# One fused kernel of attention, expert layer and dense layer on one core: all weight splits on VectorE, quarter rows stored in the dense layer's second half, weight conversions in tighter marks, the third split behind the logits' copies

## The chip, the cores and the metric

The kernel runs on one core of a Trainium2 chip. The metric is the device time of one execution in microseconds (us): the median of three timed runs. A separate profiled execution gives the trace from which all rows below are taken. The engines are named as the profile names them: PE is TensorE (with its weight loads as PEld), DVE is VectorE, ACT is ScalarE, POOL is GpSimd, and SP is SyncE, which here only issues transfers.

## The reference, cut to what matters

```python
# attention with a sigmoid: B=4, H=12, S=448, D=64
scores = q @ k.T / sqrt(D) - log(S)
x = (sigmoid(scores) @ v) -> rows of 768, N = 1792 tokens
# expert layer: E=8 experts, 768 -> 1024 -> 768, one expert per token
logits = x @ w_gate; e = argmax(logits); g = softmax(logits)[e]
y = g * (relu(x @ w1[e]) @ w2[e])
# dense layer: 768 -> 2048 -> 768
out = relu(y @ w_in) ** 2 @ w_out
```

All arithmetic is at fp32 accuracy. The kernel gets it from three fast matmuls for each product: a matrix a is split into a high part h, its value rounded to the matmul's type, and a low part l = a - h, and a product is h·h + h·l + l·h.

## The kernel before

**Attention.** 24 units (four batches, six pairs of heads each) run one after the other. In unit n PE computes the scores in four chunks, ACT the sigmoids, and PE the product with v of unit n-1 (`av_step`), its transposes (`rows`, called by `extras`) and, in every third unit, gate logits (`logits`, `token_logits`). DVE splits the next unit's q and k (`split_qk`, tiles qkh and qkl), copies results out of PSUM (xT, ls, lg) and converts the dense layer's weights.

**Conversion of the dense weights.** They come as 64-bit floats in 16 pieces of 128x1536 and are turned into 32-bit floats on DVE by `narrow(m, k)`: step 0 loads, steps 1 to 4 make the bits (step 2 also has an absolute value on ACT, tile ca or whc, which step 4 reads), and a write to DRAM follows on POOL's queue (w_d for m < 8; t_d for the eight pieces of the second layer, behind steps 5 and 6, which form sums for a seven-product block scheme). Pieces 0 to 8 (`PRE` = 9) are converted in the attention: `convert(n, half)` is called twice in each unit. Pieces 9 to 15 are converted in the dense layer's first half by `rest()`, which is called four times in each `layer1` and has one buffer wlc for its result, so step 1 of the next piece waits until the write of the last one has landed.

**Expert layer.** Routing (`head`, `counts`, `slots`, `late_places`, ...) puts the tokens into 15 slots of 128 rows with one expert each (`NBASE`) and four quarters of 32 rows. A slot takes eight weight chunks c: four for the first matrix (`up`), four for the second (`down`). PE works through them in order. Once it has done chunk c of slot s, `next_chunk(s, c)` splits chunk c of slot s+1: h on ACT, l on DVE, and for c = 7 (`POOL_W`) and s < 13 l on POOL. The four transposed parts of the hidden layer are split by `htrans` (ACT hh, DVE hl); PE needs hl for its third matmul of `down(4)`. Slot 0's chunks are split by `split_first` (chunks 0 to 3) and by `opening`.

**Quarters.** Their results wait in yq_d and are copied into y_d, at row numbers that the routing computes, by `quarter_rows()`: four times a register load and a transfer of 32x769 on POOL's queue. As the rows aren't known in advance, such a transfer waits for all earlier reads and writes of y_d.

**Dense layer.** Two blocks of tokens (8 tiles, then 6). Each runs 16 calls of `layer1` (first half), then seven products of four steps g each with weights from t_d (second half). y_d's tiles are loaded by `load_y` on SP and transposed by `trans_y`; those of block 1 are loaded from g = 16 of block 0 on.

The order on each engine is the program's order (the schedule is manual); every engine and every DMA queue takes its instructions in that order and stands still while the first of them waits.

Of the kernel before, what the change touches and what calls it, by code (L numbers as in the profile page):

```python
# [10 lines left out]
F32 = mybir.dt.float32  # L11
# [6 lines left out]
ALU = mybir.AluOpType  # L18
# [25 lines left out]
NBASE = NTL + 1  # L44
NCOL = FS + LC
QB = 3
CH = 1536
# [5 lines left out]
DH = DM // 2  # L53
PRODS = (0, 2, 6, 5, 7, 4, 3)
PRE = 9
POOL_W = (7,)
TWO30 = 2.0 ** 30
TINY = 2.0 ** -15 * 1.125

# [1 line left out]
def f32(ap):  # L61
    return ap.bitcast(F32)
# [3 lines left out]
def moe_kernel(ctx: ExitStack, tc: tile.TileContext, qk, v, wg, wm, w2, out):  # L66
    nc = tc.nc
# [119 lines left out]
    def head(t0, t1):  # L187
        n = t1 - t0
        l, q, m_, me_ = lg[:, t0:t1], eq[:, t0:t1], m[:, t0:t1], me[:, t0:t1]
        mb = m_.unsqueeze(2).to_broadcast([CP, n, E])  # L190
        V.tensor_reduce(out=m_, in_=l, op=ALU.max, axis=AX.X)
        V.tensor_tensor(q, l, mb, op=ALU.is_equal)
        V.tensor_tensor(z[:, t0:t1], l, mb, op=ALU.subtract)
        V.tensor_tensor(q, q, rev[:CP].unsqueeze(1).to_broadcast([CP, n, E]), op=ALU.mult)
        V.tensor_reduce(out=me_, in_=q, op=ALU.max, axis=AX.X)
        V.tensor_tensor(oh.rearrange("p e t -> p t e")[:, t0:t1], q, me_.unsqueeze(2).to_broadcast([CP, n, E]), op=ALU.is_equal)
        V.tensor_tensor_scan(cum[:CP].rearrange("p e t -> p (e t)"), seg[:CP].rearrange("p e t -> p (e t)"), ohz[:CP].rearrange("p e t -> p (e t)"), 0.0,
                             op0=ALU.mult, op1=ALU.add)
# [120 lines left out]
    def rtile(k, name, dt=F32):  # L319
        return rawp.tile([128, 2 * CH], dt, tag=f"raw{k}", name=name)  # L320
# [4 lines left out]
    with ExitStack() as actx:  # L325
# [83 lines left out]
        def token_logits():  # L409
            if not ready_l:  # L410
                return
            b, ls = ready_l.pop(0)
            o = lgT[b][:CP, S:S + NC * E].rearrange("p (c e) -> p c e", c=NC)
            for c in range(NC):
                nc.tensor.matmul(o[:, c], ls[:GJ * GW, c * CP:(c + 1) * CP], pick[:GJ * GW], start=True, stop=True, skip_group_check=True)
            nc.vector.tensor_copy(lg[:, b * NC:(b + 1) * NC, :], o)
# [19 lines left out]
        cvp = cctx.enter_context(tc.tile_pool(name="cvp", bufs=2, reuse_waits="tile"))  # L436
        conv = {}

        def convert(n, half):
            if n < 2:  # L440
                if half == 0:
                    fetch(n)
                return
            m, o = divmod(n - 2, 2)
            if m < 0 or m >= PRE:
                return
            if o == 0 and half == 0:
                conv[m] = (conv[m], cvp.tile([128, 2 * CH if m >= 8 else CH], F32, tag="dst", name=f"cd{m}"),
                           cvp.tile([128, CH], F32, tag="ab", name=f"ca{m}", bufs=1))
            narrow(m, 1 + 2 * o + half, *conv[m])  # L450
            if o == 1 and half == 0 and m + 2 < PRE:
                fetch(m + 2)
            if o and half:
                narrow(m, 5, *conv[m])
            if (m == PRE - 1 if o and half else o == 0 and half == 0 and m > 0):
                last = m if o else m - 1
                narrow(last, 6, *conv.pop(last))

        def fetch(m):
            conv[m] = cvp.tile([128, 2 * CH], F32, tag="src", name=f"cs{m}")  # L460
            narrow(m, 0, conv[m], None, None)
# [6 lines left out]
                    fin_av(b, j, po)  # L468
                    done.append((b, j))

        def split_w(src, h, l, pool=False):
            nc.scalar.activation(h, src, AF.Copy)  # L472
            (nc.gpsimd if pool else nc.vector).tensor_tensor(l, src, f32(h), op=ALU.subtract)  # L473

        def split_first(c):
            split_w(chunk0(c), wh[c], wl[c])
            if c == 1:
                for w, l in (("wh", wh), ("wl", wl)):
                    both = wpair(w, F32R, f"{w}23")
                    l.extend([both[:, :CH], both[:, CH:]])  # L480
# [3 lines left out]
        for n, (b, j) in enumerate(units):  # L484
            if n + 3 < len(units):
                loaded[n + 3] = load(*units[n + 3])
            if n == 0:
                nc.sync.dma_start(out=gw[:, :, :E], in_=wg)
                nc.sync.dma_start(out=x_d[0:128, :].rearrange("p (a n) -> p a n", a=8), in_=zero.unsqueeze(1).to_broadcast([128, 8, DM // 8]))
                nc.sync.dma_start(out=g_d[:FR].rearrange("(a t) b -> a (t b)", a=1), in_=zero[0:1, :FR])  # L490
            if n >= len(units) - 4:
                rawb.append(rtile(n % 4, f"raw{n}"))
                raw.extend([rawb[-1][:, :CH], rawb[-1][:, CH:]])
            if n == last_n - 3:
                cctx.close()
                w1p = ctx.enter_context(tc.tile_pool(name="w1p", bufs=1, side="right", reuse_waits="tile"))
                wh, wl = ([w1p.tile([128, CH], F32R, tag=f"{w}{c}", name=f"{w}{c}") for c in range(2)] for w in ("wh", "wl"))
                first = wpair("wl", F32, "first")
            if n == last_n - 2:
                regs(0)  # L500
                reload(0, 0)
                reload(0, 1)
            if n == last_n - 1:
                reload(0, 2)
                reload(0, 3)
            if n == last_n:
                reload(0, 4)
                reload(0, 5)
            vr = loaded.pop(n)[1]
            if n + 1 < len(units):  # L510
                terms[n + 1] = split_qk(n + 1)
            r = terms.pop(n)
            po = ps_a.tile([128, 512], F32, tag="po", name=f"po_{b}_{j}")
            cur = [score(b, j, 0, r), score(b, j, 1, r)]
            due = len(ready_l)
            if done:
                logits(*done[0])
            av_step(0)
            av_step(1)
            av_step(2)  # L520
            convert(n, 0)
            cur.append(score(b, j, 2, r))
            cur.append(score(b, j, 3, r))
            if due or n == last_n - 4:
                token_logits()
            if n == last_n - 3:
                p1 = ps_e.tile([128, 512], F32, tag="lgT", name="p1")
                pn1, prk1 = p1[:, :E], p1[:CP, E:E + FR * E].rearrange("p (e t) -> p e t", e=E)
                pr1 = p1[:, E + FR * E:E + FR * E + 2 * FS]
                counts(pn1, prk1, FR)  # L530
            if done:
                extras()
            if n == last_n - 2:
                pick_rows(pr1, Bt1, FR)
            av_step(3)
            if n == last_n - 4:
                head(0, FR)
            convert(n, 1)
            if n == last_n - 3:
                early_expert(pn1, prk1)  # L540
                spots(range(FR))
            if n == last_n - 2:
                early_rest(pr1)
                xg = {s: early_gather(s) for s in range(FS)}
            if n == last_n - 1:
                split_first(0)
            if n == last_n:
                split_first(1)
                split_first(2)
            prev = (b, j, cur, vr, po)  # L550
        av_step(0)
        av_step(1)
# [8 lines left out]
        logits(*done[0])  # L561
        extras()
        token_logits()
        head(FR, NR)
        split_first(3)
        nc.scalar.activation(ez[:, :FR], z[:, :FR], AF.Exp)
# [87 lines left out]
    with ExitStack() as mctx:  # L654
# [25 lines left out]
            nc.tensor.matmul(ps, lh, rl, start=False, stop=False)  # L680
            nc.tensor.matmul(ps, ll, rh, start=False, stop=last)  # L681

        def split_m(c, pool):
            split_w(raw[c], mh[c], ml[c], pool=pool)

        def next_chunk(s, c):
            if s + 1 < NBASE:
                split_m(c, c in POOL_W and s < NBASE - 2)
            if s + 2 < NBASE:
                reload(s + 2, c)  # L690
            if s == NBASE - 2:
                load_next(min(c + 1, AHEAD))
# [319 lines left out]
    for bi, (t0, P) in enumerate(blocks):  # L1012
# [52 lines left out]
        for c, h in steps:  # L1065
            layer1(c, h)
            if bi == 0 and c < 2 and h == 0:
                for t in (2 * c, 2 * c + 1):
                    trans_y(0, 1, t, yns.pop(t), yT[1], ps_q, ("pq", "pq"))
                    if t + 2 < P:  # L1070
                        yns[t + 2] = load_y(0, 1, t + 2, xgp, 2, "xg")
                if c == 0:
                    quarter_rows()
            seen[c] = seen.get(c, 0) + 1
            if seen[c] == 2:
                second(c)
                advance()
            if len(seen) == 8 and sum(seen.values()) == 15:
                split_s(0)
                split_s(1)  # L1080
        if bi == 0:
            ob = [rtile(k, f"ob{k}") for k in (2, 3)]
        obs = [[ob[h][:, p * DM:(p + 1) * DM] for p in range(P)] for h in range(2)]
        po = {}
# [118 lines left out]
```

## Time and profile before

| | us |
|---|---|
| median of three timed runs | 977.54 (977.25 to 978.46) |
| the profiled execution, its own time | 974.72 |
| its span, first to last instruction | 972.9 |
| PE busy | 939.6 (97% of the span) |
| DVE busy | 634.5 (65%) |
| ACT busy | 551.0 (57%) |
| POOL busy | 132.8 (14%) |

Attention fills the span up to about 184 us, the expert layer up to about 506 us, and the dense layer the rest. The profiled execution is 2.82 us below the median of the timed runs. "Busy" of PE counts matmuls as they overlap, so 97% doesn't mean that the array runs at its peak; what counts for a change here is where PE stands still, and at which clock it runs afterwards.

### The profile page before, as it was taken

The page shows a single profiled execution, that of the slowest core. Times are in us where ns is not written, and L with a number is a line of the kernel's source. Part 1 is how long each engine was busy: PE and PEld are TensorE (multiplying, and loading weights), DVE is VectorE, ACT ScalarE, POOL GpSimd, SP SyncE. Part 2 cuts the span into 40 slices and gives each one's busy share as a digit, 9 for nine tenths or more (in the row PEclk, how much of TensorE's full clock was granted, in tenths as well). Part 3 has the DMA queues.
Part 4 walks back from the last instruction along what each step waited for, and adds up shares of the span by engine and source line. Part 5 has one row for each costly group of instructions (what it writes and reads, how often), then busy time and mean ns, then how long its engine had stood idle before and what let it go on. Part 6 is the DMA issues. An engine that isn't in the chain of part 4 may idle for free. (4 is left out here: it accounts for less than half of the span.)

```text
span 972.9 us, 15008 instructions
## 1 busy us (share of the span) xinstructions
PE 939.6 (97%) x5869; PEld 786.3 (81%) x5869; DVE 634.5 (65%) x694; ACT 551.0 (57%) x667; POOL 132.8 (14%) x118
## 2 busy tenths in 40 slices
PE   7999999998999999999989799999999999999996
PEld 3555554587888888888878588889999999999996
DVE  2777777789876777777755486647866612228762
ACT  4766665756777777777854255455435344446540
POOL 1000001024523333222200100000000210000002
PEclk9999999999999999999999899999999999999998
DMA  8798868571577879593545555463233532223312
GB/s 283 255 339 300 297 231 313 182 298 37 174 281 276 333 252 387 202 408 117 202 158 193 189 208 202 187 226 99 98 123 123 192 115 65 66 66 105 123 33 97
DMA packets 52511, 190.62 MB, mean 196 GB/s; under 512 B 8082, under 2 KB 18962, under 8 KB 50386
## 3 DMA queue, kind: packets, MB, share of 16 engines
q1 hardware_dynamic: 34290, 152.77, 43.8%
q0 software_dynamic: 6928, 31.08, 8.4%
q10 hardware_dynamic: 11216, 5.75, 2.1%
q8 instruction: 48, 0.79, 0.3%
q14 instruction: 29, 0.24, 0.1%
HBM read 203.33 MB, written 36.98 MB: 247 GB/s over the span
## 5 line engine op out<-in xcount | busy, mean ns | idle before, releaser
L473 DVE TENSOR_TENSOR wl<-raw,wh 128x1536 fp32r<-128x1536 f32 x98 | 195.5, 2000 | 59.7 <-ACT wh L472 56.3
L472 ACT ACTIVATE wh<-raw 128x1536 fp32r<-128x1536 f32 x110 | 163.0, 1483 | 2.7 <-PE ph L681 0.6
L377 ACT ACTIVATE a<-sc,bias_s 128x896 f32<-128x896 f32 x96 | 82.6, 911 | 56.6 <-PE sc L373 56.3
L1036 ACT ACTIVATE r<-pp 128x512 f32<-128x512 f32 (+1 forms) x64 | 34.9, 545 | 100.5 <-PE pp L1032 100.2
L1134 PE MATMUL pq<-wrh,sh 128*128 128x384 f32 x264 | 89.1, 337 | 0.3 <-DVE ob L1095 0.3
L1135 PE MATMUL pq<-wrl,sh 128*128 128x384 f32 x264 | 88.7, 336 | 0.0
L1136 PE MATMUL pq<-wrh,sl 128*128 128x384 f32 x264 | 88.7, 336 | 0.0
L681 PE MATMUL py<-wh,hl 128*128 128x384 f32 x240 | 81.8, 341 | 5.5 <-DVE hl L706 5.5
L679 PE MATMUL py<-wh,hh 128*128 128x384 f32 x240 | 85.2, 355 | 0.0
L680 PE MATMUL py<-wl,hh 128*128 128x384 f32 x240 | 81.3, 339 | 0.0
L473 DVE TENSOR_TENSOR wrl<-raw,wrh 128x1536 fp32r<-128x1536 f32 x30 | 52.7, 1758 | 36.1 <-ACT wrh L472 36.1
L679 PE MATMUL ph<-wh,xh 128*128 128x512 f32 x180 | 74.9, 416 | 0.0
L472 ACT ACTIVATE wrh<-raw 128x1536 fp32r<-128x1536 f32 x30 | 44.4, 1483 | 48.6 <-PE pq L1136 43.3
L681 PE MATMUL ph<-wh,xl 128*128 128x512 f32 x180 | 71.2, 396 | 0.0
L680 PE MATMUL ph<-wl,xh 128*128 128x512 f32 x180 | 71.1, 395 | 0.0
L1057 DVE TENSOR_TENSOR sl<-h,sh 128x1024 fp32r<-128x1024 f32 (+1 forms) x56 | 59.8, 1086 | 8.7 <-ACT sh L1056 8.6
L1044 DVE TENSOR_TENSOR h<-h,h 128x512 f32<-128x512 f32 (+1 forms) x16 | 10.0, 624 | 80.7 <-ACT h L1039 80.7
L383 PE MATMUL po<-a,qkv 128*64 128x448 f32 x288 | 59.6, 548 | 0.0
L473 POOL TENSOR_TENSOR wl<-raw,wh 128x1536 fp32r<-128x1536 f32 x12 | 42.0, 3497 | 128.5 <-ACT wh L472 128.4
L1056 ACT ACTIVATE sh<-h 128x1024 fp32r<-128x1024 f32 (+1 forms) x56 | 51.5, 943 | 13.5 <-PE pq L1135 8.0
L1000 POOL DMA_INDIRECT out<-ob,idx x14 | 13.7, 978 | 314.7 <-DVE ob L1095 286.0
L1030 PE MATMUL pp<-hy,wrh 128*128 128x512 f32 (+1 forms) x132 | 49.5, 375 | 6.8 <-ACT r L1036 6.8
(290 smaller groups left out, 2192.2 us busy)
## 6 DMA issues: line engine op xcount, KB each, us to landing
raw<-in_wm SPq DMA_DIRECT2D x110, 768.0 KB
qraw<-in_wm SPq DMA_DIRECT2D x32, 768.0 KB
raw<-t_d SPq DMA_DIRECT2D x28, 768.0 KB
cs<-in_w SPq DMA_DIRECT2D x9, 1536.0 KB
raw<-w_d SPq DMA_DIRECT2D x16, 768.0 KB
qkv<-in_qk SPq DMA_DIRECT2D x23, 480.0 KB
whc<-in_w SPq DMA_DIRECT2D x7, 1536.0 KB
t_d<-wlc POOLq DMA_DIRECT2D x7, 1536.0 KB, 7.7
```

Of the source, the lines that this page charges most:

```text
L377: nc.scalar.activation(a[:, :n], ps[:, :n, :S], AF.Sigmoid, bias=bias_s, scale=1.0 / math.sqrt(D))
L383: nc.tensor.matmul(po[64 * h:64 * h + 64, :S], vr[:, 128 * c + 64 * h:128 * c + 64 * h + 64], a[:, h], start=(c == 0), stop=False, skip_gr ...
L472: nc.scalar.activation(h, src, AF.Copy)
L473: (nc.gpsimd if pool else nc.vector).tensor_tensor(l, src, f32(h), op=ALU.subtract)
L679: nc.tensor.matmul(ps, lh, rh, start=first, stop=False)
L680: nc.tensor.matmul(ps, lh, rl, start=False, stop=False)
L681: nc.tensor.matmul(ps, ll, rh, start=False, stop=last)
L1056: nc.scalar.activation(sh[:, :2 * N], src, AF.Copy)
L1057: V.tensor_tensor(sl[:, :2 * N], src, f32(sh[:, :2 * N]), op=ALU.subtract)
L1134: nc.tensor.matmul(po[p][:, :DH], lh, wc[:, w0:w0 + DH], start=(q == 0 and kk == 0 and o in (0, 2, 5)), stop=False, **fl)
L1135: nc.tensor.matmul(po[p][:, :DH], lh, wcl[:, w0:w0 + DH], start=False, stop=False, **fl)
L1136: nc.tensor.matmul(po[p][:, :DH], ll, wc[:, w0:w0 + DH], start=False, stop=(q == 3 and kk == 1), **fl)
```

## The change

Four edits:

1. `next_chunk` gives no split to POOL any more. Chunk 7's l is made on DVE, as that of the other chunks; these are 12 instructions.
2. `quarter_rows()` is called after the last `layer1` of block 0, where it was called after the first.
3. The conversion steps of pieces 0 to 8 in the attention follow a list of marks, two for each unit. Step 1 of every even piece but the first shares a mark with step 4 of the piece before it, steps 5 and 6 of piece 8 have a mark each, and the last mark lies in unit 18 (before: unit 19). The number of steps is the same.
4. `split_first(2)` moves from the end of unit 23 to behind `token_logits()`, ahead of the second `head`.

```diff
+        marks = []
+        for i in range(PRE):
+            for k in range(1, 5):
+                if i and i % 2 == 0 and k == 1:
+                    marks[-1].append((i, k))
+                else:
+                    marks.append([(i, k)])
+        marks.extend([[(PRE - 1, 5)], [(PRE - 1, 6)]])
+
         def convert(n, half):
             if n < 2:
                 if half == 0:
                     fetch(n)
                 return
...
+            for m, k in marks.pop(0) if marks else ():
+                if k == 1:
+                    conv[m] = (conv[m], cvp.tile([128, 2 * CH if m >= 8 else CH], F32, tag="dst", name=f"cd{m}"),
+                               cvp.tile([128, CH], F32, tag="ab", name=f"ca{m}", bufs=1))
+                narrow(m, k, *conv[m])
+                if k == 3 and m + 2 < PRE:
+                    fetch(m + 2)
...
-        def split_w(src, h, l, pool=False):
+        def split_w(src, h, l):
             nc.scalar.activation(h, src, AF.Copy)
-            (nc.gpsimd if pool else nc.vector).tensor_tensor(l, src, f32(h), op=ALU.subtract)
+            nc.vector.tensor_tensor(l, src, f32(h), op=ALU.subtract)
...
                 split_first(1)
-                split_first(2)
             prev = (b, j, cur, vr, po)
...
         token_logits()
+        split_first(2)
         head(FR, NR)
         split_first(3)
...
-                split_m(c, c in POOL_W and s < NBASE - 2)
+                split_m(c)
...
-                if c == 0:
-                    quarter_rows()
             seen[c] = seen.get(c, 0) + 1
...
         if bi == 0:
+            quarter_rows()
             ob = [rtile(k, f"ob{k}") for k in (2, 3)]
```

How the rows move on three engines and places. First POOL's queue in the dense layer, from the fourth quarter on (the other three read the same); t_d is the write of a converted piece, out the scatter of finished rows. Before:

```order
L1005 TENSOR_LOAD ctl
L1005 ISA x2
L1006 ISA
L1006 DMA y_d<-yq_d 32x769
L131 DMA t_d<-wlc 128x8x384 x7
L1000 DMA out<-ob_7552,idx_82 1792x768 x4
```

Now, from the conversions' writes on to the first quarter:

```order
L130 DMA t_d<-wlc 128x8x384 x7
L1006 TENSOR_LOAD ctl
L1006 ISA x2
L1007 ISA
L1007 DMA y_d<-yq_d 32x769
```

The seven writes of pieces 9 to 15 stood behind the four quarters and stand ahead of them now.

Second DVE at the end of the attention: wl are low parts of slot 0's weights (the first row here is chunk 2's), xl those of its tokens, and the rows that begin with m<-lg are the second `head`, which ends with cum. Before:

```order
L473 TENSOR_TENSOR wl_1772<-raw_1466,wh_1771 128x1536
L299 TENSOR_TENSOR xl_1782<-tx_1779,xh_1781 128x512
L299 TENSOR_TENSOR xl_1782<-tx_1780,xh_1781 128x256
L390 COPY xT_5_1796<-po_5_1718 128x448
L406 COPY ls_1811<-lgT_1677 96x448
L416 COPY lg<-lgT_1677 112x32
L191 TENSOR_REDUCE m<-lg 112x4
```

Now:

```order
L298 TENSOR_TENSOR xl_1780<-tx_1777,xh_1779 128x512
L298 TENSOR_TENSOR xl_1780<-tx_1778,xh_1779 128x256
L389 COPY xT_5_1794<-po_5_1718 128x448
L405 COPY ls_1809<-lgT_1677 96x448
L415 COPY lg<-lgT_1677 112x32
L474 TENSOR_TENSOR wl_1772<-raw_1466,wh_1771 128x1536
L190 TENSOR_REDUCE m<-lg 112x4
```

Chunk 2's split left its place ahead of xl, xT, ls and lg and stands ahead of `head`. On ACT its high part moved in the same way, from ahead of xh to behind the last xn.

Third DVE between slots 1 and 2, behind the last row of `late_routing` (gp); wl_1870 is chunk 7's, wl_1473 and wl_1474 are chunks 0 and 1's. Before:

```order
L832 CAST gp<-gr 112x16
L473 TENSOR_TENSOR wl_1473<-raw_1466,wh_1471 128x1536
L473 TENSOR_TENSOR wl_1474<-raw_1466,wh_1472 128x1536
L706 TENSOR_TENSOR hl_2318<-pht_0_2374,hh_2317 128x512
L473 TENSOR_TENSOR wl_1772<-raw_1562,wh_1771 128x1536 x2
```

Now:

```order
L833 CAST gp<-gr 112x16
L474 TENSOR_TENSOR wl_1870<-raw_1715,wh_1866 128x1536
L474 TENSOR_TENSOR wl_1473<-raw_1466,wh_1471 128x1536
L474 TENSOR_TENSOR wl_1474<-raw_1466,wh_1472 128x1536
L707 TENSOR_TENSOR hl_2318<-pht_0_2374,hh_2317 128x512
```

Three splits stand ahead of hl where two stood; the third was on POOL behind three products Bg. PE's rows keep their order everywhere.

## Rows read from the trace of the kernel before

**Rows 1.** Waits by engine: waiting line, releaser; us in total, times, longest.
```profile
PE pp L1030 <- ACT r L1036: 6.8, 1, 6.8
PE py L681 <- DVE hl L706: 5.5, 3, 4.6
PE lgT L401 <- DVE xT L390: 1.5, 1, 1.5
```

**Rows 2.** Timeline of POOL, dense layer: start, us, instruction, [idle before <-releaser].
```profile
529.26 0.56 POOL L1006 DMA_DIRECT2D y_d<-yq_d  x1 [38.08 <-DMA yn<-y_d]
...
538.12 0.95 POOL L131 DMA_DIRECT2D t_d<-wlc  x1
```

**Rows 3.** Timeline of DVE, dense layer: piece 9's last step, piece 10's first.
```profile
525.71 0.56 DVE L130 TENSOR_TENSOR wlc<-wlc 128x384 f32<-128x384 f32 x1
...
544.55 0.96 DVE L112 TENSOR_SCALAR wlc<-whc 128x1536 uint32<-128x1536 uint32 x1 [10.76 <-issue]
```

**Rows 4.** Timeline of ACT, dense layer: piece 10's absolute value.
```profile
547.34 1.76 ACT L115 ACTIVATE whc<-whc 128x1536 f32<-128x1536 f32 x1 [11.57 <-DVE wlc L114]
```

**Rows 5.** Timeline of PE, dense layer.
```profile
510.04 0.80 PE L1032 MATMUL pp<-yt,wrl 128*128 128x512 f32 x1 [2.38 <-issue]
...
549.63 0.80 PE L1030 MATMUL pp<-hy,wrh 128*128 128x512 f32 x1 [6.76 <-ACT r L1036]
```

**Rows 6.** Windows: length, busy us of each engine, then PE's granted clock.
```profile
549.60:554.00 4.40, 4.37 (x10) 3.48 (x11) 3.41 (x5) 1.74 (x3) 0.62 (x1) 0.50 0.46 140
237.00:240.20 3.20, 3.16 (x10) 3.14 (x11) 3.20 (x2) 0.00 (x0) 2.10 (x2) 0.54 0.47 136
510.00:513.10 3.10, 3.06 (x7) 2.47 (x8) 3.03 (x4) 0.00 (x0) 0.00 (x0) 0.51 0.89 361
```

**Rows 7.** Timeline of SP: the first loads of block 1's rows.
```profile
725.08 1.32 SPq L617 DMA_DIRECT2D yn<-y_d  x2
```

**Rows 8.** Timeline of DVE, slot 2.
```profile
228.78 7.61 DVE L473 TENSOR_TENSOR wl<-raw,wh 128x1536 fp32r<-128x1536 f32 x2
```

**Rows 9.** Timeline of POOL, slot 2: the third Bg, then chunk 7's split.
```profile
228.96 2.28 POOL L836 TENSOR_TENSOR Bg<-Bs,gp 112x384 bf16<-112x384 f16 x1 [0.62 <-DVE gp L832]
...
231.33 3.43 POOL L473 TENSOR_TENSOR wl<-raw,wh 128x1536 fp32r<-128x1536 f32 x1
```

**Rows 10.** Timeline of PE, slot 2.
```profile
237.04 0.69 PE L681 MATMUL py<-wh,hl 128*128 128x384 f32 x1 [4.56 <-DVE hl L706]
```

**Rows 11.** Timeline of DVE, a later slot.
```profile
274.06 5.39 DVE L473 TENSOR_TENSOR wl<-raw,wh 128x1536 fp32r<-128x1536 f32 x2 [2.91 <-ACT wh L472]
279.37 0.68 DVE L706 TENSOR_TENSOR hl<-pht,hh 128x512 fp32r<-128x512 f32 x1
```

**Rows 12.** Timeline of PE, the same slot: the first matmul with hl.
```profile
280.63 0.34 PE L681 MATMUL py<-wh,hl 128*128 128x384 f32 x1
```

**Rows 13.** Timeline of DVE, units 19 and 20: piece 8's step 4, next qkh.
```profile
148.02 1.73 DVE L119 SCALAR_TENSOR_TENSOR cd<-ca,cd 128x1536 f32<-128x1536 f32 x1
...
151.79 0.65 DVE L360 CAST qkh<-qkv 128x960 fp32r<-128x960 f32 x1
```

**Rows 14.** Timeline of PE, unit 21's first scores.
```profile
152.59 0.47 PE L373 MATMUL sc<-qkh 64*128 64x448 f32 x2 [0.68 <-DVE qkh L360]
153.69 0.48 PE L373 MATMUL sc<-qkl,qkh 64*128 64x448 f32 x2 [0.64 <-DVE qkl L361]
```

**Rows 15.** Timeline of DVE, end of the attention: chunk 2's split; head's first and last row.
```profile
178.57 1.76 DVE L473 TENSOR_TENSOR wl<-raw,wh 128x1536 fp32r<-128x1536 f32 x1
...
184.71 0.19 DVE L191 TENSOR_REDUCE m<-lg 112x4 f32<-112x32 f32 x1
...
185.94 0.44 DVE L197 TENSOR_TENSOR_SCAN cum<-seg,ohz 112x136 bf16<-112x136 bf16 x1
```

**Rows 16.** Timeline of ACT, the same place: the first split behind the last xn.
```profile
184.39 1.49 ACT L472 ACTIVATE wh<-raw 128x1536 fp32r<-128x1536 f32 x1 [0.39 <-ACT xn L423]
```

**Rows 17.** Timeline of PE, the same place: the first matmul that reads cum.
```profile
186.49 0.18 PE L201 MATMUL r<-cum,ones 112*128 112x8 bf16 x1
```

More of the change, by code (lines that the diff above doesn't have):

```diff
@@ L55 @@
 PRE = 9
-POOL_W = (7,)
 TWO30 = 2.0 ** 30
@@ L443, in convert @@
                 return
[L444 to L457, printed above, removed]
+            for m, k in marks.pop(0) if marks else ():
[5 more added lines that the diff above has]
+                    fetch(m + 2)
         def fetch(m):
@@ L681, in mm3, with split_m @@
             nc.tensor.matmul(ps, ll, rh, start=False, stop=last)
-        def split_m(c, pool):
-            split_w(raw[c], mh[c], ml[c], pool=pool)
+        def split_m(c):
+            split_w(raw[c], mh[c], ml[c])
         def next_chunk(s, c):
             if s + 1 < NBASE:
-                split_m(c, c in POOL_W and s < NBASE - 2)
+                split_m(c)
             if s + 2 < NBASE:
```

## The prediction, made before the result was known

> **What bounds the kernel now.** I read the table of waits first, because PE is busy nearly all the time and only its standstills, and the slow clock behind them, can be taken away. PE waits long in few places [rows 1]: 6.8 us once in the dense layer's first half, 5.5 us in three waits for hl (one of 4.56 [rows 10], the others small), 1.5 us for the last xT; two waits of 0.68 and 0.64 us stand between units 20 and 21 [rows 14]. Then the timelines of POOL, DVE, ACT and PE at each of these places, followed back to what was late, and the windows for the granted clock. Outside those places PE goes from one matmul to the next, so an engine that only gets less work there gains nothing.
>
> What the reader is to see in the largest stall: POOL stood 38.08 us at the first quarter's transfer, because that had to wait for the reads of y_d [rows 2]. Piece 9's result was ready at 525.71 + 0.56 = 526.27 [rows 3], but its write stood behind the four quarters and was issued at 538.12 [rows 2]. Piece 10's first step needs wlc back: DVE idled 10.76 us up to 544.55 [rows 3]. ACT waited 11.57 us with the absolute value [rows 4], the relu stood behind that on ACT, and PE waited 6.76 us for the relu [rows 5]. When it came back it ran 4.4 us at a granted clock of 0.50, the 1.2 GHz level [rows 6].
>
> **Part 1, quarter rows.** The first conversion write no longer stands behind them. It can be issued at 526.3, 11.8 us sooner. From issue to piece 10's first step it was 544.55 - 538.12 = 6.4 us; so that step may begin at 532.8, say 534 behind other DVE work. The absolute value ran from 547.34 to 549.10, 2.8 to 4.6 us behind that step; it would now end near 538.6. In the old run PE ran dry at 549.63 - 6.76 = 542.9, so the relu behind it has over 4 us of room, and a write that lands 4 us later than I assume still costs nothing. Saved: 6.8 us of wait, and half of the 4.4 us at half clock, 2.2 us. **-9.0 us.** From below, if another conversion step were late next: 0; from above -9.0, since no other wait hangs on it. The quarters themselves go to POOL behind the last conversion write. The next reader of y_d is the load at 725.08 [rows 7]; four transfers, which took 538.12 - 529.26 = 8.9 us with their waits [rows 2], begin more than 70 us before it. If that cover were gone, the price would be those 8.9 us.
>
> **Part 2, conversions end in unit 18.** In unit 19 DVE did step 4 to 6 of piece 8 from 148.02 and came to unit 21's qkh only at 151.79 [rows 13], 3.8 us later than it could. PE waited 0.68 + 0.64 us [rows 14]. With those steps done a unit before, qkh can start at about 148.0, and both waits go: **-1.3 us** (nothing else at this place can gain; 0 from below). The steps are the same in number, two marks for each unit; four marks (pieces 2, 4, 6 and 8) carry a further step 1 of 0.96 us [rows 3]. I cost that at nothing, because PE reads qkh and qkl only a unit later; without the cover it is at most 4 x 0.96 = 3.8 us.
>
> **Part 3, the third split.** Chunk 2's split took DVE's 1.76 us ahead of xl and the last xT [rows 15]. PE's 1.5 us for that xT go [rows 1], and all up to the logits' copies comes 1.5 us sooner. But the split now stands ahead of `head`, and its high part on ACT stands behind the last xn, where the next split began at 184.39 [rows 16]. Shifted: high part 182.9 to 184.4, low part to 186.15, then `head`, which took from 184.71 to 186.38 [rows 15], ends at 187.8. PE wants cum 1.5 us sooner than 186.49 [rows 17], at 185.0. A new wait of 2.8 us takes the place of the old one: **+1.3 us** net, before its clock. Queued behind that wait on PE are the rest of slot 0 and all that follows; nothing hides it. Bounds: -1.5 if cum were there in time, +2.8 if the gain ahead of it failed.
>
> **Part 4, splits off POOL.** In slot 2 two splits of DVE took 7.61 us in place of 3.5 [rows 8]: the second could run only once POOL had ended Bg (at 231.24) and its own split (at 234.76) [rows 9]. Then came hl, and PE waited 4.56 us [rows 10]. Now DVE has three splits there: the first until 230.5, Bg until 231.24, two more until 234.8, hl (0.68 us [rows 11]) until 235.4 in place of 237.0. **-1.6 us**, between 0 (a further clash) and -4.56. The slow clock behind the old wait, 3.2 us at 0.54 [rows 6], cost 1.5 us. In the other eleven slots I take nothing: DVE had 2.91 us of idle time ahead of the pair [rows 11], into which the added 1.76 us fit, and PE, which needs hl at 280.63 [rows 12] and had it at 280.05, didn't wait.
>
> Here a rule can be weighed. The pair in the later slot took 5.39 us for 3.5 us of work [rows 11]: a split on POOL takes about as much from DVE as it saves. The Trainium skill, SBUF — State Buffer, section "Who interferes with whom", says that a DVE instruction with two inputs in SBUF contends with a GpSimd instruction that reads SBUF and that the loser blocks fully; the trace agrees, with 7.61 us. [...]
>
> **The clock behind the waits that stay.** Two waits of 2.8 and 3.0 us remain, the new one and slot 2's. After a wait of 2.38 us the clock stood at 0.51 for 3.1 us [rows 5, 6], which costs 1.5 us; PE had stood still shortly before it too. After the 1.5 us wait no slow stretch shows. So each costs 0 or 1.5 us; these waits lie nearest to the 2.38 us, but it isn't certain, and I take one of the two: **+1.5 us**, both ends kept.
>
> **Sum.** -9.0 - 1.3 + 1.3 - 1.6 - 1.5 + 1.5 = -10.6 us. From the profiled execution's own 974.72 us that makes 964.1; from the median, 2.82 us above it, 966.9. I forecast the median.
>
> **Rivals.**
> - *VectorE is late in every slot* (the other side). Place: hl at the end of `up`; the price is 1.76 us less the 0.58 us of room (280.63 - 280.05), twelve times: +14.2 us, 981.1. For it: DVE is busy most of the slot. Against it: the idle 2.91 us and the clash that goes. It decides where DVE's idle time ahead of the pair is under 1.76 us. Chance 4%. [...]
> - *Slot 2's wait doesn't shrink*: three splits and another clash with POOL's gather leave hl at 237.0. Then part 4 gives 0, with the old clock loss, and the new wait costs its 1.5 too: -9.0 - 1.3 + 1.3 + 1.5 = -7.5, 970.0. For it: POOL's next instruction is a gather. Chance 13%.
> - *The stall moves on* (the change doesn't do what it says): the relu is late for another reason, say the load of piece 10 or the landing of the write, and half of the 9.0 us stays: 971.4. Against it: over 4 us of room. Chance 6%.
> - *The denser marks hold the attention up* by up to 3.8 us: 970.7. For it: DVE is the next busiest engine there. Chance 6%.
>
> **How the numbers follow.** The forecast with its clock cases (-9.1 with both slow, -12.1 with none) has 71%: 965.4 to 968.4, with a margin of a microsecond or two for the bounds of parts 3 and 4. The three middle rivals reach to 971.4. If the wait for cum or slot 2's wait vanished altogether, -15 would come: 962.5. The range is 962.8 to 971.4; it leaves out the slower rival and mixtures. 0.2% of the time, 2 us, is about what a measurement of this kernel can tell from no change. Faster by more: all but the first rival and mixtures, 94%; within: 3%; slower: 3%.
>
> **What would show each step.** Part 1: PE has no wait at `layer1` of over 1 us behind the dense layer's first one, POOL's first conversion write follows DVE's last step at once, and the load of block 1's rows doesn't wait. Part 2: unit 20 follows 19 without a wait for qkh. Part 3: the wait for xT is gone and a wait of about 2.8 us ahead of L201 is there, released by DVE's cum. Part 4: splits on DVE take 1.76 us in the mean, and slot 2's wait is near 3.0 us. Wrong if PE shows a new wait for hl in every slot, or the first half of the dense layer still stands still.

## The result and the profile after

The changed kernel takes 963.58 us (median of four runs, 962.59 to 964.05), the kernel before 977.41 beside it on the same chip (977.25 to 978.46). The ratio is 0.9855 with a 95% interval of 0.9838 to 0.9872: 13.8 us by the medians, where I had forecast 10.6 and a time of 966.9. The profiled execution took 963.18 us with a span of 961.7; that is 11.5 below the one of before.

PE's waits in the changed kernel (waiting line, releaser; us in total, times, longest):

```profile
PE r L200 <- DVE cum L196: 2.9, 1, 2.9
PE py L682 <- DVE hl L707: 2.7, 1, 2.7
PE pp L1032 <- issue: 2.6, 1, 2.6
PE ph L680 <- ACT xn L422: 1.6, 1, 1.6
```

Of [rows 1] the 6.8 us for the relu and the 1.5 us for xT are gone, and the 5.5 us for hl are 2.7. The waits of [rows 14] don't appear either. The wait for cum that I forecast is there; the one of 1.6 us behind xn I had not seen coming.

**Part 1 in the trace.** POOL, then DVE, then ACT in the dense layer (start, us, instruction, idle before and its releaser), and below them windows over the stretch in which PE had stood still (length, busy us of PE, PEld, DVE, ACT, POOL, then PE's granted clock):

```profile
524.35 0.97 POOL L130 DMA_DIRECT2D t_d<-wlc  x1 [35.80 <-DVE wlc L129]
```

```profile
523.49 0.56 DVE L129 TENSOR_TENSOR wlc<-wlc 128x384 f32<-128x384 f32 x1
...
531.49 0.95 DVE L111 TENSOR_SCALAR wlc<-whc 128x1536 uint32<-128x1536 uint32 x1
```

```profile
534.27 1.65 ACT L114 ACTIVATE whc<-whc 128x1536 f32<-128x1536 f32 x1 [0.72 <-DVE wlc L113]
```

```profile
520.00:545.00 25.00, 25.00 (x116) 20.50 (x115) 14.24 (x26) 10.67 (x21) 1.87 (x2) 1.00 0.61 235
545.00:560.00 15.00, 15.00 (x67) 12.27 (x66) 13.57 (x13) 9.10 (x11) 0.00 (x0) 1.00 0.54 193
```

The write follows DVE's last step within 0.3 us (524.05 to 524.35; 11.9 us in [rows 2, 3]). Piece 10's first step begins 7.1 us behind the write with no idle time noted ahead of it, and PE is busy all the 40 us at full clock. The quarters now go out on POOL behind the last conversion write:

```profile
627.40 0.55 POOL L1007 DMA_DIRECT2D y_d<-yq_d  x1 [0.80 <-issue]
...
643.16 0.50 POOL L1007 DMA_DIRECT2D y_d<-yq_d  x1 [4.01 <-DMA y_d<-yq_d]
```

That is 15.8 us from the first to the last on POOL's queue, more than the 8.3 of before (529.26 to 537.59), and it costs nothing: the load that reads behind them, on SP, is issued 70 us later without a wait.

```profile
714.04 0.99 SPq L618 DMA_DIRECT2D yn<-y_d  x2
```

**Part 3 in the trace.** The end of the attention: PE, ACT and DVE.

```profile
182.03 0.50 PE L680 MATMUL ph<-wh,xh 128*128 128x512 f32 x1 [1.60 <-ACT xn L422]
...
187.27 0.17 PE L200 MATMUL r<-cum,ones 112*128 112x8 bf16 x1 [2.88 <-DVE cum L196]
```

```profile
181.38 0.60 ACT L422 ACTIVATE xn<-pt 112x512 f32<-112x512 f32 x1 [3.43 <-DMA x_d<-xn]
...
182.36 2.86 ACT L473 ACTIVATE wh<-raw 128x1536 fp32r<-128x1536 f32 x2 [0.39 <-ACT xn L422]
```

```profile
183.88 1.76 DVE L474 TENSOR_TENSOR wl<-raw,wh 128x1536 fp32r<-128x1536 f32 x1 [3.23 <-ACT wh L473]
...
186.77 0.44 DVE L196 TENSOR_TENSOR_SCAN cum<-seg,ohz 112x136 bf16<-112x136 bf16 x1
```

The chain is the forecast one (last xn, high part, low part, `head`, PE), but it starts late: xn has two buffers, and ACT stood 3.43 us until the transfer out of one of them had landed.

**Part 4 in the trace.** Slot 2, DVE and then PE:

```profile
229.85 5.74 DVE L474 TENSOR_TENSOR wl<-raw,wh 128x1536 fp32r<-128x1536 f32 x3
235.52 0.68 DVE L707 TENSOR_TENSOR hl<-pht,hh 128x512 fp32r<-128x512 f32 x1
```

```profile
236.25 0.44 PE L682 MATMUL py<-wh,hl 128*128 128x384 f32 x1 [2.73 <-DVE hl L707]
```

Three splits take 5.74 us where two took 7.61 [rows 8]; PE waits 2.73 us where it waited 4.56 [rows 10].

### The profile page after: what moved, and what is told of

Its sections match the earlier page's. It is cut to its first block, busy times and chain, and to the rows that moved or that the text cites. A ratio compares the mean times of both kernels' runs of the same rounds, so it can differ in the third digit from the quotient of the medians.

```text
span 961.7 us, 15015 instructions
## 1 busy us (share of the span) xinstructions
PE 935.9 (97%) x5869; PEld 784.7 (82%) x5869; DVE 631.2 (66%) x706; ACT 551.4 (57%) x667; POOL 78.8 (8%) x106
## 5 line engine op out<-in xcount | busy, mean ns | idle before, releaser
L474 DVE TENSOR_TENSOR wl<-raw,wh 128x1536 fp32r<-128x1536 f32 x110 | 192.6, 1761 | 63.8 <-ACT wh L473 62.0
L1134 PEld LDWEIGHTS pq<-wrh,sh 128*128 128x128 f32 x264 | 49.6, 188 | 0.6 <-issue 0.6
L1135 PEld LDWEIGHTS pq<-wrl,sh 128*128 128x128 f32 x264 | 49.6, 188 | 0.0
L1136 PEld LDWEIGHTS pq<-wrh,sl 128*128 128x128 f32 x264 | 49.6, 188 | 0.0
```

What stands on the lines that cost most here:

```text
L474: nc.vector.tensor_tensor(l, src, f32(h), op=ALU.subtract)
L1134: nc.tensor.matmul(po[p][:, :DH], lh, wc[:, w0:w0 + DH], start=(q == 0 and kk == 0 and o in (0, 2, 5)), stop=False, **fl)
L1135: nc.tensor.matmul(po[p][:, :DH], lh, wcl[:, w0:w0 + DH], start=False, stop=False, **fl)
L1136: nc.tensor.matmul(po[p][:, :DH], ll, wc[:, w0:w0 + DH], start=False, stop=(q == 3 and kk == 1), **fl)
```

## The experiments

Unless another kernel is named, a difference is one of medians against the kernel before on the same chip, with the difference that the 95% interval of the ratio gives in brackets.

### Each edit alone

Edit 2 alone, the quarter rows:

```diff
-                if c == 0:
-                    quarter_rows()
...
         if bi == 0:
+            quarter_rows()
```

> The kernel before with only the quarter rows moved behind the last layer1 of block 0. Theory (POOL's queue held up the conversions): the 6.8 us wait at layer1 and the slow clock behind it go, 9.0 us less than the kernel before; POOL's first conversion write comes under 0.2 us behind DVE's last step. Rival (the stall moves on to the next late conversion): under 5 us less, with a wait of 2 us or more left on PE in the first half of the dense layer.

966.66 against 976.67: -10.0 us (-8.8 to -11.8). PE's wait for the relu is gone from its list and the others stand as before. The first conversion write is issued 0.3 us behind DVE's last step (527.50 to 527.80), a little more than the 0.2 expected. Part 1 holds.

Edit 3 alone, the marks:

```diff
+            for m, k in marks.pop(0) if marks else ():
...
+                narrow(m, k, *conv[m])
```

> Edit 3 alone (the list of marks), everything else as before. My theory: the two waits of 0.68 and 0.64 us for qkh and qkl between units 20 and 21 go, and the unit starts about 0.5 us sooner, so that the end of the attention comes 1.3 to 2.2 us sooner and the time falls by 1.3 to 2.2 us. Rival one, that steps which share a mark hold the attention up elsewhere: no gain or up to 3.8 us more. Rival two, that the single edits add up: both kernels of the first batch that had edits 1 and 2 alone gave -4.5 and -10.0 us, and the version without edit 4 gave -16.9, which would leave -2.4 us for this edit.

973.42 against 976.89: -3.5 us (-2.1 to -4.2). The waits for qkh and qkl are gone and the wait for the last xT comes 2.0 us sooner (at 179.83, where PE's row stands at 181.84 in the trace of before); 0.4 of this is already there at unit 20's beginning (143.82 against 144.19). So the trace shows some 1.65 us from the marks, of which 1.32 are the two waits. The time says more than that, and more than the 2.2 us at most that I expected; the 2.4 of the second rival lie in the interval. Executions of equal clock point to PE's clock for the rest: the eight executions of this kernel with a mean granted clock of 0.990 have a median of 973.1 us, the nine such of the kernel before (profiled ones and other chips included) 974.7, which are 1.6 us; most executions of the kernel before had 0.987 or less. No run tests this reading.

Edit 4 alone, the third split:

```diff
                 split_first(1)
-                split_first(2)
...
         token_logits()
+        split_first(2)
         head(FR, NR)
```

> The kernel before with only chunk 2's split moved behind the logits' copies. Theory (head stands behind the split and ACT's last xn behind a transfer): PE waits about 2.9 us for cum and about 1.6 us for xn, in place of 1.5 us for xT; 2.5 to 4.5 us more than before. Rival (the forecast's size, no wait for xn): 1.3 us more, 2.8 with a slow clock. Second rival (the edit helps): 1.5 us less.

978.06 against 976.67: +1.4 us (+0.5 to +2.2), the only edit that makes the kernel slower, and the size of the forecast's term. My expectation of 2.5 to 4.5 us fails, and its first rival holds. PE in this kernel, and the window behind the wait:

```profile
187.04 0.18 PE L201 MATMUL r<-cum,ones 112*128 112x8 bf16 x1 [2.64 <-DVE cum L197]
```

```profile
187.00:190.20 3.20, 3.16 (x10) 2.59 (x10) 2.92 (x10) 0.99 (x2) 0.00 (x0) 0.52 0.00 0
```

The wait of 1.47 us for xT is exchanged for one of 2.64 (forecast: 2.8), and 3.2 us at 0.52 of the clock follow. Here ACT did not wait for a transfer ahead of its last xn and PE not for xn, so what the changed kernel's profile shows on top of this isn't edit 4's in every execution.

Edit 1 alone, the splits off POOL, here by an empty list of the chunks that go there:

```diff
-POOL_W = (7,)
+POOL_W = ()
```

> The kernel before with all splits of the slots on DVE and nothing else changed. Theory (a split on POOL and one on DVE take turns): slot 2's wait for hl falls from 4.56 to about 2.8 us, and the slow clock behind it may go; 1.6 to 3.2 us less than before, and the mean of DVE's splits in the slots falls from 2.00 to about 1.76 us. Rival (DVE is late in every slot): up to 14 us more, with waits for hl in most slots.

972.19 against 976.67: -4.5 us (-3.5 to -6.2), more than the 1.6 to 3.2 expected. The mean of DVE's 110 splits is 1761 ns, where 98 splits took 2000 before; DVE's busy time over the whole span falls by 3 us, to 631.5, although it has 12 splits more:

```profile
L473 DVE TENSOR_TENSOR wl<-raw,wh 128x1536 fp32r<-128x1536 f32 x110 | 192.5, 1761 | 60.7 <-ACT wh L472 59.0
```

The four single edits add to -16.6 us by the medians, the whole change gave -13.8. The intervals of the five comparisons are wide enough for both; I don't read an interaction from it.

### All but the third split

The changed kernel with `split_first(2)` put back to the end of unit 23:

```diff
                 split_first(1)
+                split_first(2)
...
         token_logits()
-        split_first(2)
         head(FR, NR)
```

> The changed kernel with chunk 2's split back at the end of unit 23, so three edits of four. Theory: the waits for cum and xn go and the one for xT comes back; 2.5 to 4.5 us less than the changed kernel's 963.6, so 959 to 961. Rival (the move pays for itself): 1 to 3 us more than the changed kernel.

959.81 against 976.67, in the 959 to 961 expected: -16.9 us; by the ratio, 0.9839, between -13.9 and -17.6. The 1.5 us for xT are back and those for cum and xn are gone. By the medians it is 3.8 below the changed kernel, but that one's interval (0.9838 to 0.9872) overlaps. That edit 4 costs something rests on the run with it alone, whose interval excludes zero.

### The same kernels again

The changed kernel and the kernel before, unaltered, each once more.

> The changed kernel once more, as the yardstick of this batch and for a second profile. Time 963.6 within 1 us. One theory: whether the clock falls behind a short wait is settled by the length of the wait, so the second profile shows the slow clock at the same two places (behind the 2.9 us for cum and behind the 2.6 us at the dense layer's start) and not behind slot 2's 2.7 us. The rival: it varies from execution to execution at the same wait, so at least one of the three places shows it the other way.

962.92 us. It has the same three waits as the first profile (2.6 for cum, 2.7 for hl, 2.9 at the dense layer's start), but the one for xn isn't there, and the clock fell in another place. Its PE, ACT and windows behind the waits for hl and cum:

```profile
185.29 0.17 PE L200 MATMUL r<-cum,ones 112*128 112x8 bf16 x1 [2.65 <-DVE cum L196]
...
234.22 0.54 PE L682 MATMUL py<-wh,hl 128*128 128x384 f32 x1 [2.73 <-DVE hl L707]
```

```profile
179.40 0.60 ACT L422 ACTIVATE xn<-pt 112x512 f32<-112x512 f32 x1 [1.43 <-PE pt L421]
```

```profile
234.20:237.40 3.20, 3.19 (x10) 3.13 (x11) 3.20 (x2) 0.00 (x0) 2.08 (x2) 0.53 0.44 138
185.30:188.50 3.20, 3.20 (x13) 2.56 (x13) 2.96 (x9) 0.93 (x2) 0.00 (x0) 0.71 0.01 3
```

The same windows of the first profile of the same program, the wait for hl again 2.73 us:

```profile
236.20:239.40 3.20, 3.15 (x19) 3.12 (x20) 3.20 (x2) 0.67 (x2) 2.12 (x2) 1.00 0.45 127
187.30:190.50 3.20, 3.20 (x10) 2.61 (x10) 2.94 (x9) 0.95 (x2) 0.00 (x0) 0.51 0.01 3
```

In 3.2 us PE did 19 matmuls in one execution and 10 in the other, behind a wait of the same length. So the rival of that expectation holds. The last xn was 2.0 us sooner here (179.40 against 181.38), because the transfer two before it had landed in time, and PE came to cum 2.0 us sooner.

> The kernel before once more, for a second profile of it: the first one's execution took 974.72 us, 2.8 below the median of the timed runs. Time 976 to 977.5. Theory: what differs between executions of one program is the clock behind the short waits and the first loads, so that at the same 1.5 us wait for the last xT, or the same 4.56 us wait for hl, the clock falls in one profile and not in the other, at about 1 us each. Rival: the waits themselves are longer in this profile.

976.35 us, ratio 1.0003. This profiled execution took 978.68 us, the first one 974.72, with none of its waits over 0.3 us longer but the very first one, for the first load (6.04 against 5.63):

```profile
PE pp L1030 <- ACT r L1036: 6.7, 1, 6.7
...
PE py L681 <- DVE hl L706: 4.9, 2, 4.6
PE pp L1032 <- issue: 2.7, 1, 2.7
PE lgT L401 <- DVE xT L390: 1.5, 1, 1.5
```

The difference begins behind the wait for the last xT: in the first profile the clock stayed at 1.00 from 183.5 to 186.5, here it is at half for 6.4 us.

```profile
184.00:187.20 3.20, 3.20 (x10) 2.64 (x11) 2.33 (x9) 3.05 (x3) 0.00 (x0) 0.50 0.29 72
187.20:190.40 3.20, 3.20 (x11) 2.28 (x10) 2.17 (x8) 0.66 (x2) 0.00 (x0) 0.54 0.00 0
```

Up to slot 2's wait for hl this makes 1.8 us. Most of the rest comes at the dense layer's start (1.4 us) and behind the relu (0.8), each time with PE longer at the low clock: in the second 3.2 us behind the wait it had 0.56 and 0.57 here, 1.00 and 0.82 in the first profile. So the program of before varies by 4 us from execution to execution without a wait that is longer by more than about 0.4 us, and the execution that I made the sum against was one of its quickest. The theory holds for the wait of 1.5 us; behind the one of 4.56 us the clock fell in both profiles (0.54 and 0.55).

### A third buffer for xn

```diff
-            xn = sp_.tile([128, NC, 128], F32, tag="xn", name=f"xn_{b}_{j}")
+            xn = sp_.tile([128, NC, 128], F32, tag="xn", name=f"xn_{b}_{j}", bufs=3)
```

> The changed kernel with a third buffer for xn, so that the last xn needn't wait for the transfer of the one two before it. My theory: that wait (3.43 us on ACT) is what made part 3 dearer than forecast. Without it the last xn runs about 2.0 us sooner, PE's wait of 1.6 us ahead of slot 0's first matmuls goes, chunk 2's split and the head behind it come 2.0 us sooner, PE still waits about 2.9 us for cum, and the time is 2.0 us below that of the changed kernel run beside it. Rival: the transfer isn't the cause (xn is late for the matmul pt): no gain, within 0.5 us.

962.21 against 962.92 of the changed kernel beside it; the expected 2.0 us are not there. The waits for xn are gone, but they were absent in the unaltered kernel's second profile as well: from the logits' copy on PE (179.49 there, 180.65 here) to cum (185.29, 186.44) both take 5.8 us, the first profile took 7.8. The theory that xn's transfer makes edit 4 dearer holds for single executions only; as a fixed price it falls. 962.21 us is not to be told from no change.

### The second head first, and the split in halves

The changed kernel with chunk 2's split behind `head`:

```diff
         token_logits()
-        split_first(2)
         head(FR, NR)
+        split_first(2)
         split_first(3)
```

> The changed kernel with chunk 2's split moved behind the second head, still ahead of chunk 3's. My theory: PE's wait of 2.9 us for cum is the split that stands ahead of head and nothing else; it goes, and the slow clock behind it (1.1 us) with it, so the time is 3 to 4 us below that of the changed kernel run beside it; PE's wait of 1.6 us behind the late xn stays. Rival: PE reads chunk 2's low part so soon that the wait comes back there, or cum is late for the late copies of the logits too: under 1.5 us gained.

962.09 us, 0.8 below the changed kernel, where I had expected 3 to 4. The wait for cum is gone, but the next one stands a few matmuls behind it:

```profile
PE pht L705 <- ACT hr L722: 2.0, 1, 2.0
```

```profile
187.28 0.18 ACT L252 ACTIVATE sa<-r 128x8 f32<-128x8 f32 x1 [1.43 <-DVE t L246]
187.36 1.47 ACT L473 ACTIVATE wh<-raw 128x1536 fp32r<-128x1536 f32 x1
188.73 0.59 ACT L722 ACTIVATE hr<-ph 128x512 f32<-128x512 f32 x1
```

ACT's first copy of the hidden layer (hr) stands behind sa, a number of the routing, which waits for DVE; DVE comes to it only after both splits that now follow `head`. I had considered what stands ahead of cum and not the counts behind it. Between sa and hr ACT also has a split of 1.47 us to do (the middle row); a version with hr ahead of that split was not run.

Then the high part on ACT at the end of unit 23, the low part on DVE behind `head`:

```diff
                 split_first(1)
+                nc.scalar.activation(wh[2], chunk0(2), AF.Copy)
...
-        split_first(2)
         head(FR, NR)
+        nc.vector.tensor_tensor(wl[2], chunk0(2), f32(wh[2]), op=ALU.subtract)
```

> The changed kernel with chunk 2's split taken apart: the high part on ACT where it was before the change (end of unit 23), the low part on DVE behind the second head. My theory: DVE carries nothing ahead of the last xT and nothing ahead of head, and ACT has no second high part ahead of hr, so of the waits for xT (1.5 us), for cum (2.6 to 2.9) and for hr (2.0 in the version with head first) none is left over 0.6 us. Time 958 to 959.5, that is 1 us below the version without edit 4 (959.81) and 3.5 to 5 below the changed kernel. Rival: the high part ahead of the tokens' xh makes xl and so the last xT late by itself, and the 1.5 us come back: 960 to 961.

960.34 us (960.04 to 961.85). The waits for xT, cum and xn are all gone, but hr's 2.0 us stand as in the version ahead of it. So I was right on three waits and wrong on the fourth: it wasn't ACT's extra split that held hr up but DVE's two ahead of sa, with ACT's 1.47 us between sa and hr as before. The time is the rival's, by another way than it named. Behind hr's wait the clock fell to 0.50 in the profile of the version ahead of it and stayed at 1.00 here. It is the best order of the third split that I tried, level with the version without edit 4 (959.81). Its runs lie below all of the changed kernel's first four (962.59 to 964.05) but not below the quickest of the later five (960.83), so that it beats the kernel before surely (0.9846, 0.9832 to 0.9859) and the changed one by some 3 us by the medians.

### Routing a slot later

The version in halves, with `late_routing` behind chunk 2 of slot 2, ahead of its second half:

```diff
+                if s == 2 and c == 2:
+                    late_routing()
...
-                if s == 1 and c == 6:
-                    late_routing()
```

> The same with late_routing behind the first half of slot 2, so that of the three splits and the 3.9 us of routing only the splits stand ahead of hl on DVE. My theory: the wait for hl of 2.7 us in slot 2, which part 4 left, goes together with the slow clock that followed it in three of six profiles (1.5 us): 2.7 to 4 us below the version with the split taken apart alone. Rival: the wait moves to the slot's end, where PE's product with Bg (pgt) now waits for the routing's gates, or to the second hl: less than 1 us gained.

965.12 us, 4.8 slower than the version in halves: my theory fails, by a way that neither it nor the rival named. Slot 2's wait for hl is gone (the 0.6 us for hl that are left are one in slot 0, which the version in halves has too), but:

```profile
PE py L681 <- DVE gp L834: 5.6, 1, 5.6
```

```profile
L925 PEldq TENSOR_LOAD <-ctl x1: 487/487/487, 236.1 to 236.1; - x1
```

In this slot PE loads a register from the routing's table ctl ahead of its second half (the number of tokens that decides on the last steps); the line above, with its least, median and longest time in ns, shows it on PE's queue at 236.1. DVE finished ctl at 236.08, and PE went on at 236.66, as soon as the 487 ns of the load were over; so PE stood 5.63 us until the routing was done. The table has a reader on PE's queue that I had overlooked. (This profile also shows the wait behind xn again, 2.0 us.)

### POOL's splits back in the late slots

The changed kernel with chunk 7's split on POOL in eleven slots, all but the one that matters to slot 2's hl:

```diff
-                split_m(c)
+                split_m(c, c == 7 and 2 <= s < NBASE - 2)
```

> The changed kernel with chunk 7's split back on POOL in eleven slots, for all but the one that is split in slot 1 (whose hl is the one that PE waited 4.56 us for). My theory: part 4 gains in that one place only, so this costs nothing: within 0.7 us of the changed kernel (963.58, 962.92), with the mean of DVE's splits back near 2.0 us. Rival: the splits on POOL held hl up in the later slots too (the run with edit 1 alone gave -4.5 us where the one wait explains some 3): 1 to 2 us slower than the changed kernel.

963.66 us, 0.1 and 0.7 above the changed kernel's two medians: as expected, nothing. DVE's and POOL's splits in it:

```profile
L474 DVE TENSOR_TENSOR wl<-raw,wh 128x1536 fp32r<-128x1536 f32 x99 | 193.7, 1963 | 60.8 <-ACT wh L473 57.6 <-DMA raw<-in_wm 0.3 <-PE py L682 0.3
...
L474 POOL TENSOR_TENSOR wl<-raw,wh 128x1536 fp32r<-128x1536 f32 x11 | 38.6, 3508 | 127.9 <-ACT wh L473 127.8
```

99 splits on DVE take 193.7 us, 110 take 192.6 in the changed kernel: eleven splits that POOL does save DVE nothing, they cost it 1.1 us. One later slot of the changed kernel, with POOL idle during its first two splits (chunks 7 and 0; chunk 1's is the row at 275.57):

```profile
270.31 3.43 DVE L474 TENSOR_TENSOR wl<-raw,wh 128x1536 fp32r<-128x1536 f32 x2 [1.28 <-ACT wh L473]
275.57 1.76 DVE L474 TENSOR_TENSOR wl<-raw,wh 128x1536 fp32r<-128x1536 f32 x1 [1.83 <-ACT wh L473]
277.25 0.68 DVE L707 TENSOR_TENSOR hl<-pht,hh 128x512 fp32r<-128x512 f32 x1
```

The same slot here, where POOL does chunk 7's split and DVE chunks 0 and 1's; the last line has the shortest, median and longest of these two in ns:

```profile
270.27 3.51 POOL L474 TENSOR_TENSOR wl<-raw,wh 128x1536 fp32r<-128x1536 f32 x1 [12.55 <-ACT wh L473]
271.86 5.39 DVE L474 TENSOR_TENSOR wl<-raw,wh 128x1536 fp32r<-128x1536 f32 x2 [2.91 <-ACT wh L473]
277.16 0.69 DVE L707 TENSOR_TENSOR hl<-pht,hh 128x512 fp32r<-128x512 f32 x1
L474 DVE TENSOR_TENSOR wl<-raw,wh x2: 1759/2652/3544, 271.9 to 275.5; 128x1536 fp32r<-128x1536 f32 x2
```

Chunk 0's split beside POOL's takes 3.54 us in place of 1.76, that is 1.78 longer, just what the split on POOL took off DVE. By the Trainium skill, SBUF — State Buffer, section "Who interferes with whom", a DVE instruction with two inputs in SBUF contends with a GpSimd instruction that reads SBUF, since its second input comes through a read interface that both share; the trace agrees, with those 1.78 us. In both kernels hl comes at the same time (277.16 and 277.25): chunk 1's split ahead of it needs ACT's high part, which is there at 275.5 in both, and by then DVE is through with chunk 0 in both. So it makes no difference in this slot where chunk 7 was split. One wait for hl that the changed kernel lacks is back in a late slot, of 0.37 us (474.25).

## Why the prediction was right

**What bounds the kernel.** Right: each wait that went without another in its place gave at least its length, and the eleven slots in which an engine only got other work gave nothing that the time shows (963.66 us).

**Part 1, -9.0.** Right in mechanism and near in size: -10.0 alone. Write, first step and absolute value came in the forecast order; the step was forecast at 534 in the old kernel's time, 27 us behind the dense layer's first matmul (506.96), and stood 27.1 behind it (531.49 - 504.36). The cover for the quarters was real: the last left POOL at 643.7, 70 us ahead of its reader.

**Part 2, -1.3.** The two waits went. The term was small by some 0.3 us in the trace; the run alone gave -3.5 (at least -2.1), of which the trace doesn't show the rest.

**Part 3, +1.3.** Right in its chain. The run alone gave +1.4, but the 1.3 stood ahead of any clock loss, and in that run's profile the clock fell behind the wait; so the match of the two numbers is partly chance. I read the waits that it would bring off the order of the instructions, and missed that xn's buffer may still be on its way out; where it is, as in the changed kernel's first profile, another 2 us come.

**Part 4, -1.6 and -1.5.** The wait fell from 4.56 to 2.73 us (forecast 3.0), and nearly all of the gain is there, as the run with eleven splits back on POOL shows. The old clock loss is not surely saved, see next. Alone the edit gave -4.5; the waits for hl, 5.5 us before and 3.3 with it, and, in executions where it doesn't come, the clock loss (1.5) explain 3.7 of it at most, near the lower end of its interval (3.5).

**The clock, +1.5.** This is where the prediction's mechanism was wrong: it took whether a wait costs "0 or 1.5 us" as something that the wait's length decides, and compared lengths. The runs show that for waits of 1.5 to 2.9 us it's settled anew in each execution. Behind slot 2's wait of 2.7 us the clock fell in four of eight profiles (granted clock in the 3.2 us behind it: 0.63 with edit 1 alone, 0.73 without edit 4, 0.53 in the changed kernel's second profile, 0.60 with eleven splits on POOL) and stayed at 1.00 in four; behind the old wait of 4.56 us it fell in all five (0.50 to 0.59). Behind the wait of 1.5 us for xT, of which I wrote that no slow stretch follows, it fell in two of six (edit 2 alone and the second profile of before). The 1.5 us that I took for two waits is about what half of the cases gives, so the sum hardly suffered; that is luck and not the reasoning.

**The sum.** -10.6 forecast, -13.8 by the medians, and the term that was mis-sized can be named: the forecast carried the 2.82 us by which the kernel before's median lay above its profiled execution over to the changed kernel. There the median lies 0.40 above the profiled execution, 2.4 less; that execution itself took 963.18 us, 0.9 less than the 964.1 forecast. Together these are the 3.3 us between 966.9 and 963.58. The 974.72 us were a quick execution of a program that ranges from 974.4 to 978.9 us, and its time goes with its clock: the nine executions with a mean granted clock of 0.990 took 974.4 to 975.7 us, the five with 0.983 took 978.4 to 978.9. That fits a usual execution of before with more slow stretches to lose than the one that I read; no run separates this from the rest, and how the 2.4 us are shared among the edits stays open. It is luck, too, that the range held: 963.58 lies below the 965.4 to 968.4 of the main case, in the margin left for the bounds of parts 3 and 4, and both of their waits are there at about the size forecast.

**The rivals.** No late hl in the later slots, so VectorE was not the bound there (chunk 0's split took 1.76 us in place of 3.54, which made up for the split that DVE got). Slot 2's wait shrank. The stall at the relu did not move on. The denser marks held nothing up.

## What to carry to other kernels

A transfer whose row numbers are known only at run time waits in this program for all earlier reads and writes of its target, and holds up all that stands behind it on its queue; put it behind the writes that others wait for, and see when its own reader comes (10 us here for moving one call). Moving a split from VectorE to GpSimd saved VectorE nothing, because its own split beside it took as much longer; look for that wherever both engines subtract tiles in SBUF at once. When a wait goes, look at the next three instructions of every engine that waited, register loads of shared tables included, before counting its length as gain: twice the next wait stood right behind (2.0 us for hr, 5.6 us for ctl).

## What the runs showed of the hardware that was not expected

- The same program with the same waits takes 974.4 to 978.9 us. Much of this is PE's clock: in the 3.2 us behind the same 2.73 us wait it was 1.00 once and 0.53 once; behind the wait for cum of 2.6 to 2.9 us it fell in four profiles (0.51 and 0.71 in the changed kernel's two) and stayed at 1.00 in a fifth (that with eleven splits on POOL, wait 2.65 us). The length of a wait between 1.5 and 2.9 us doesn't tell which; behind the longer ones (4.56 us, five profiles; 6.7 to 6.9 us, five) it always fell. What else decides stays open.
- DVE's subtraction of two 128x1536 tiles took 1.76 us alone and 3.54 us beside one of GpSimd.
- A transfer out of SBUF may take long enough to hold the buffer's next writer 3.43 us in one execution and not at all in the next.
- The gathers of the slots' tokens on POOL take 1278 ns in the mean in the changed kernel and 2204 ns where eleven splits stand on POOL ahead of them. They are hidden here; the cause is open.
